# Two layers of SSM convolution and GEGLU on one core: DFT tables with half samples, and two filter blocks transformed by even and odd tokens between the layers' matmuls

## The chip, the core and the metric

The kernel runs on one core of a Trainium2 chip. The metric is device time in microseconds of one launch; the kernel before takes 943.9 us (median of 3 runs, 942.08 to 944.71). Its engines are named as in the profile: PE (TensorE's matmuls) and PEld (its weight loads), DVE (VectorE), ACT (ScalarE), POOL (GpSimd) and SP (SyncE, which here only issues DMAs). Each engine takes its own instructions in the order in which they were issued.

## What is computed

Two layers, each a gated long convolution over 2048 tokens and 576 channels and then a GEGLU feed-forward layer of width 4608. The inputs are bf16.

```python
def _A_ref(q, k, v, shift_k, ssm_k, ssm_D):        # ks = 4 taps
    k_shift = sum(k_pad[:, t:t + S, :] * shift_k[:, ks - 1 - t] for t in range(ks))
    kv = k_shift * v
    y = irfft(rfft(pad(kv, 2*S)) * rfft(pad(ssm_k, 2*S)))[:S]     # causal convolution, 2048 taps
    y = y + kv * ssm_D
    return q * y
def _B_ref(x, w_gate, w_up, w_down):
    return (_gelu(x @ w_gate) * (x @ w_up)) @ w_down

x = A_q
x = x + _A_ref(_layernorm(x), A_k, A_v, A_shift_k, A_ssm_k, A_ssm_D)
x = x + _B_ref(_layernorm(x), B_w_gate, B_w_up, B_w_down)
x = x + _A_ref(_layernorm(x), A_k, A_v, A_shift_k, A_ssm_k, A_ssm_D)
x = x + _B_ref(_layernorm(x), B_w_gate, B_w_up, B_w_down)
```

The convolution's y depends on k, v and the filter alone, so both layers share it.

## The kernel before

**Convolution.** The sequence is cut into four blocks of 512 tokens. The filter (with ssm_D added to its first tap) and kv are cut in the same way, and each block is taken to 512 frequencies by matmuls with sine tables that the kernel makes itself. Frequencies come in four tiles of 128 (`kt` 0 to 3), each with two parts `s`; tokens come as four rows `i` of 128 partitions. Output block m is the sum over blocks a of K[a] times H[m-a], a complex product on DVE (`prod`), and an inverse transform (`inverse`, L254) of 8 matmuls for each of four token tiles. Spectra wait in DRAM (`Hd` for the filter, `Kd` for kv).

Three tables are made before the feed-forward starts. `G` (1024 columns per row i) serves the filter: its token rows are contiguous, p + 128 i, which is what a DMA transpose from DRAM (`load_h`, L493) delivers. `F1` serves kv, whose token rows are interleaved, 4 p + i, and half of the inverse; `F2` serves the other half. `G`'s angles are made on DVE (`angles`, L117) and those of `F1` and `F2` on ACT (`f_angles`, L560); ACT makes the sines (L125).

There are two ways forward. `fwd_h` (L182) and `fwd_full` (L191) make one frequency tile and part from 8 matmuls of 288 columns. `fwd_eo` (L202) makes even and odd rows apart, 4 matmuls for 288 channels; sum and difference of the two (`cross`, L214) give the tiles kt and kt+2, so a block takes 8 groups of 4 where `fwd_h` takes 8 groups of 8.

**Start-up** (`begin`, L476, written out by hand). Filter block 0 is turned by TensorE transposes, blocks 1 to 3 by DMA transposes on SP's queue. Then come, on TensorE: filter block 0 (4 tiles), block 1 (tiles 0 and 2), kv block 0 by `fwd_full` (`kfwd`), the rest of block 1, block 2, the inverse of block 0, chunk 0's gate, norm and TensorE transposes (`gate0`, `root0`, `norm0`, `turn0`, `copy0`) mixed with the last tiles of blocks 2 and 3. k arrives for block 0 with its shifted rows from DRAM, in three DMAs (L141 to L143). The first 8 of block 1's 16 kv operations are done here (`kv1_ops`).

**Feed-forward.** Four chunks of 512 tokens in two layers are eight units, ordered (0,c0) (0,c1) (1,c0) (1,c1) (0,c2) (0,c3) (1,c2) (1,c3), and run in passes of 1, 2, 2, 2 and 1 units. A pass goes through F in three phases; a unit in a phase is here called a visit, so there are 24 (0 to 23). A visit has 216 gate/up matmuls (gu, L1116: 12 f-tiles of 18; each takes 64 rows, two lie side by side in the array) and 96 down matmuls (dn, L1132). ACT takes the gelu and DVE the product hT (L1121) of each f-tile; DVE adds each dn tile to x.

**What lies between.** The rest of the convolution (blocks 1 to 3, `step`, L275) and the norms are laid between these matmuls by a planner at build time. It keeps a clock per engine (`Pace`), costs for each operation (`C_...`) and queues: `Pq` for TensorE groups, `V` for DVE, `U` for the crosses after an even/odd group, `L` for loads, `aq` for ACT's statistics. After each f-tile and each dn step `fill` issues what fits. What it decides is fixed in the instruction order; TensorE takes convolution groups between f-tiles while `hurry` holds, and always between dn steps. `hurry` is over once chunk 1's y is there.

For a new unit, `prep` issues per token tile j: a product with y, a sum with x that also adds up its elements, a Square on ACT with the mean `nm` (from POOL, L834) as bias, the root on POOL, the norm `xn` on DVE (L903), and two DMA transposes on SP (`spread`, L933) that make xnT for gu.

Of the kernel before, what the change touches and what calls it, by code (L numbers as in the profile page):

```python
# [34 lines left out]
C_AC, C_AB = 0.76, 0.76  # L35
C_TT, C_ST, C_BN, C_NORM, C_HT, C_GELU, C_EVA, C_EVD = 0.76, 0.82, 0.47, 0.62, 0.69, 0.6, 0.66, 0.76
# [20 lines left out]
class Conv:  # L57
# [9 lines left out]
    def __init__(self, tc, ctx, pace, A_k, A_v, A_shift_k, A_ssm_k, A_ssm_D, ident, psp, cpsp, ypool):  # L67
# [6 lines left out]
        self.ident, self.psp, self.cpsp, self.ypool = ident, psp, cpsp, ypool  # L74
# [7 lines left out]
        self.prp = pool("c_pr", 3)  # L82
# [5 lines left out]
        self.F1 = self.cst.tile([P, RT, 2, 2, P], BF16, name="F1")  # L88
        self.F2 = self.cst.tile([P, 2, 2, 2, P], BF16, name="F2")
# [14 lines left out]
        self.V, self.L, self.Pq = deque(), deque(), deque()  # L104
# [12 lines left out]
    def angles(self, j, col, row, eng):  # L117
        for s, off in enumerate((3 * N4 // 4, 0)):
            eng.tensor_scalar(out=j[:, s, :], in0=col, scalar1=row, scalar2=float(off), op0=ALU.mult, op1=ALU.add)
# [8 lines left out]
    def load_k(self, b, eng):  # L128
# [10 lines left out]
        if b == 0:  # L139
            self.nc.vector.memset(k[0:1, 0:H, :], 0.0)  # L140
            eng.dma_start(out=flat[16:P, :], in_=rows(16 * RT + r0, P - 16))  # L141
            self.nc.gpsimd.dma_start(out=flat[1:16, :], in_=rows(RT + r0, 15))
            self.nc.gpsimd.dma_start(out=k[0:1, H:H + RT, :], in_=self.k2[0:RT, :].unsqueeze(0))  # L143
        else:
            eng.dma_start(out=flat[:], in_=rows(r0, P))
# [35 lines left out]

    def fwd_h(self, G, src, kt, s, dst):  # L182
        nc = self.nc
        ps = self.ps()
        for n, i in enumerate((2, 3, 0, 1)):
            for h in range(2):
                nc.tensor.matmul(ps[:, h, 0:HW], lhsT=G[:, i, s * NFQ + kt * P: s * NFQ + (kt + 1) * P],  # L187
                                 rhs=src[:, i, h * HW:(h + 1) * HW], start=(n == 0), stop=(n == RT - 1))
        nc.scalar.activation(out=self.halves(dst[:, s, :]), in_=ps[:, :, 0:HW], func=ACT.Copy, scale=1.0 / NFQ)

    def fwd_full(self, src, neg, kt, s, dst):  # L191

        nc = self.nc
        ps = self.ps()
        for i in range(RT):
            x = src[:, i, :] if kt < 2 or i % 2 == 0 else neg[:, i // 2, :]
            for h in range(2):
                nc.tensor.matmul(ps[:, h, 0:HW], lhsT=self.F1[:, i, s, kt % 2, :],  # L198
                                 rhs=x[:, h * HW:(h + 1) * HW], start=(i == 0), stop=(i == RT - 1))
        nc.scalar.copy(out=self.halves(dst[:, s, :]), in_=ps[:, :, 0:HW])  # L200

    def fwd_eo(self, src, kt, s, h):  # L202
# [3 lines left out]
        for e in range(2):  # L206
            for i in (e, e + 2):
                nc.tensor.matmul(ps[:, e, 0:HW], lhsT=self.F1[:, i, s, kt, :],  # L208
                                 rhs=src[:, i, h * HW:(h + 1) * HW], start=(i == e), stop=(i == e + 2))
        eo = self.eop.tile([P, 2, HW], F32, tag="eo", name="eo")  # L210
        nc.scalar.copy(out=eo[:], in_=ps[:, :, 0:HW])  # L211
# [39 lines left out]
    def lhs(self, kt, s, mt, F2):  # L251
        return self.F1[:, 2 * kt, s, mt // 2, :] if mt % 2 == 0 else F2[:, kt, s, mt // 2, :]
# [22 lines left out]
    def step(self, m, kv=None, loaded=False):  # L275
# [10 lines left out]
        if not loaded:  # L286
# [7 lines left out]
            self.L.append((lambda: self.kv_at.get(m - 1, NEVER), lk))  # L294
            self.L.append((lambda: self.fwd_at.get(m - 1, NEVER), lv))
# [34 lines left out]
        for kt, a in pairs:  # L330
            self.L.append((lambda a=a: max(self.hr_free[self.nhr % N_HR] if (m, a) != (1, 0) else 0.0,
                                           self.kr_free[self.nkr % 3] if a < m else 0.0),
                           load(kt, a)))
# [77 lines left out]
        for kt, a in pairs:  # L411
            for part in range(2):
                keys = [("ld", kt, a)] + ([("kc", kt % 2, s, h) for s in range(2) for h in range(2)] if a == m else [])
                self.V.append((lambda g=get(*keys): max(g(), self.pr_slot()), C_PR, v(kt, a, part)))
                if a > 0:
                    self.V.append((eo_done if a == 1 else lambda: 0.0, C_AC, add(kt, a, part)))
# [3 lines left out]
        for kt in range(2):  # L420
            for s in range(2):
                for h in range(2):
                    self.Pq.append((lambda: max(get("kv")(), NEVER if self.neo >= N_EO else 0.0), 0.49, fwd(kt, s, h)))
        def inv(mt):
            def run():
                self.yb = nyb
                self.inverse(m, mt, [(self.lhs(kt, s, mt, self.F2), z[(s, kt, mt % 2)])
# [8 lines left out]

    def pr_slot(self):
        return self.pr_free[self.npr % N_SM]

    def run_loads(self):  # L440
        t = self.t
        self.flush(t.pe)
        while self.L and self.L[0][0]() <= t.pe - 0.3:
            self.L.popleft()[1]()

    def run_v(self, limit):

        t = self.t
        if self.U and self.U[0][0] <= t.pe + 0.2 and max(t.dve, t.pe - 1.0) + self.U[0][1] <= limit:
# [26 lines left out]
    def begin(self, gate0, root0, norm0, turn0, copy0, x0_stats, more, scratch, wide, stay):  # L476

        tc, nc, D = self.tc, self.nc, self.D
        with ExitStack() as es:
            tmp = es.enter_context(tc.tile_pool(name="s_tmp", bufs=1))  # L480
            hp = es.enter_context(tc.tile_pool(name="s_h", bufs=2))
            sk1 = hp.tile([1, D, self.KS], BF16, tag="h", name="sk1")
            dvec = tmp.tile([1, D], BF16, name="dvec")
            ones = tmp.tile([1, P], BF16, name="ones")
            nc.vector.memset(ones[:], 1.0)
            nc.scalar.dma_start(out=sk1[:].rearrange("p d j -> p (d j)"), in_=self.sk.rearrange("d j -> (d j)").unsqueeze(0))
# [734 lines left out]
```

## Time and profile before

| What | us |
|---|---|
| Median of 3 runs | 943.9 |
| Profiled execution, its own time | 943.32 |
| Its span, first to last instruction | 941.5 |
| First gu matmul | 62.7 |
| PE busy in 0 to 20, 20 to 40, 40 to 60 | 15.48, 19.44, 16.46 |
| DVE busy in the same | 17.71, 19.29, 17.10 |
| ACT busy in the same | 16.34, 18.13, 12.15 |
| PE idle in 175 to 200 | 1.05 |

The profile lists each engine's busy time, the waits with the instruction that ended them, and the chain of work that ended last, followed back from the end. A line of the chain gives its start, its length and the instruction or DMA that the time belongs to. The busy time of an engine is no measure of what it is worth to shorten it: only work on that chain moves the end. The granted clock reads 1.00 throughout.

### The profile page before, as it was taken

Reading aid. Unit: us, or ns where it says so; the run is one execution under the profiler, and the core shown is the slowest. Engines: PE = TensorE matmul, PEld = TensorE weight load, DVE = VectorE, ACT = ScalarE, POOL = GpSimd, SP = SyncE. Lnnn points to the kernel's source line nnn. Section 1 sums busy time; section 2 is a strip of 40 time slices with the busy share of each in tenths; the row PEclk is TensorE's granted clock in tenths of the full one; section 3 lists DMA queues with packets and bytes.
Section 4 is the critical chain, followed back from the end, with each engine's and each line's share of the span. In section 5 each row is a group of like instructions: output and inputs, shape, how many; then the busy total and the mean of one; then the engine's idle time right before and its main releaser. Section 6 shows DMA issues by size and latency. Waiting matters only on the chain.

```text
span 941.5 us, 19061 instructions
## 1 busy us (share of the span) xinstructions
PE 926.9 (98%) x8128; PEld 536.5 (57%) x8128; DVE 571.4 (61%) x1027; ACT 295.9 (31%) x541; POOL 143.2 (15%) x303
## 2 busy tenths in 40 slices
PE   7989999999999999999999999999999999999998
PEld 5755564665655646546546556556556556556555
DVE  8977887898898637988982333663333335523332
ACT  8846214432124334231222421441221223311211
POOL 2453100511123104230100100230000002100000
PEclk9999999999999999999999999999999999999999
DMA  7989986765953522983930630891630630797720
GB/s 184 323 238 274 293 183 148 133 162 142 226 190 64 113 77 52 195 212 87 221 107 2 133 94 26 136 156 39 129 99 1 129 98 14 135 206 155 147 65 26
DMA packets 129065, 127.46 MB, mean 135 GB/s; under 512 B 45587, under 2 KB 121684, under 8 KB 128980
## 3 DMA queue, kind: packets, MB, share of 16 engines
q1 hardware_dynamic: 119904, 90.85, 45.7%
q0 software_dynamic: 8944, 34.49, 11.4%
q8 instruction: 63, 1.03, 0.5%
q10 hardware_dynamic: 132, 0.91, 0.4%
q14 instruction: 22, 0.18, 0.1%
HBM read 105.58 MB, written 10.62 MB: 123 GB/s over the span
## 4 chain that ended last, share of the span: by engine, by line
PE 91%; DMA 3%; DVE 2%; POOL 2%; ACT 1%; issue 1%; SPq 0%; POOLq 0%; DVEq 0%
PE gu L1116 59%; PE dn L1132 27%; DMA h<-in_A_ssm_k_dram 2%; PE cps L208 1%; PE cps L261 1%; PE ps L187 1%; DMA k<-in_A_k_dram 1%; POOL rstd L850 1%; PE ps L198 1%; DVE x_c L1161 0%; PE cps L187 0%; POOL ve L849 0%; ACT junk L842 0%; DVE x_c L877 0%; DMA xnT<-xn 0%
## 5 line engine op out<-in xcount | busy, mean ns | idle before, releaser
L1116 PE MATMUL gu<-xnT,wgu 64*128 64x512 bf16 x5184 | 565.5, 376 | 2.1 <-DVE x_c L1161 1.0
L1116 PEld LDWEIGHTS <-wgu 64*128 64x128 bf16 x5184 | 254.3, 94 | 305.2 <-issue 10.1
L1120 ACT ACTIVATE ga<-gu 128x512 f32<-128x512 f32 x288 | 171.9, 597 | 549.9 <-PE gu L1116 541.1
L1121 DVE TENSOR_TENSOR hT<-ga,gu 128x512 bf16<-128x512 f32 x288 | 197.6, 686 | 221.2 <-ACT ga L1120 219.7
L1132 PE MATMUL dn<-wd,hT 128*128 128x288 bf16 x2304 | 291.0, 286 | 0.5 <-DVE ob L1141 0.5
L1132 PEld LDWEIGHTS <-hT 128*128 128x128 bf16 x2304 | 223.5, 98 | 66.1 <-issue 10.5
L1166 DVE TENSOR_TENSOR x_c<-x_c,dn 128x576 f32<-128x576 f32 x64 | 48.2, 753 | 82.3 <-PE dn L1132 82.0
L834 POOL TENSOR_SCALAR nm<-s 128x1 f32<-128x1 f32 x60 | 21.1, 352 | 344.1 <-DVE x_c L1161 215.1
L842 ACT ACTIVATE junk<-x_c,nm 128x576 bf16<-128x576 f32 x48 | 37.0, 771 | 40.8 <-POOL nm L834 40.8
L327 POOL DMA_DIRECT2D hr<-Hd x32 | 17.3, 541 | 161.2 <-DVE prod L228 161.2
L850 POOL TENSOR_TENSOR rstd<-ve,neghalf_t 128x1 f32<-128x1 f32 x60 | 39.9, 665 | 5.0
L229 DVE TENSOR_TENSOR sum<-prod 128x576 bf16<-128x576 bf16 x72 | 33.0, 458 | 2.5
L187 PEld LDWEIGHTS <-G 128*128 128x128 bf16 x256 | 25.5, 100 | 11.2 <-issue 2.2
L187 PE MATMUL ps<-h,G 128*128 128x288 bf16 x192 | 27.6, 298 | 2.5 <-DMA h<-in_A_ssm_k_dram 1.7
L1152 DVE TENSOR_TENSOR ob<-x_c,dn 128x576 bf16<-128x576 f32 x15 | 11.2, 753 | 27.2 <-PE dn L1132 19.0
L163 DVE TENSOR_TENSOR kvt<-k,skc 128x1152 bf16<-128x1152 bf16 x32 | 23.9, 754 | 0.5
L849 POOL TENSOR_SCALAR ve<-ss 128x1 f32<-128x1 f32 x60 | 18.1, 301 | 32.4 <-ACT junk L842 32.3
L216 DVE TENSOR_TENSOR kc<-eo 128x288 bf16<-128x288 f32 x48 | 19.2, 453 | 2.1 <-ACT eo L211 2.1
L877 DVE SCALAR_TENSOR_TENSOR x_c<-g_t,rstd,x_c 128x576 f32<-128x576 f32 x16 | 13.1, 818 | 12.0 <-POOL rstd L850 11.9
L211 ACT COPY eo<-cps 128x576 f32<-128x576 f32 x24 | 15.3, 636 | 15.2 <-PE cps L208 12.7
L269 POOL DMA_DIRECT2D out_dram<-ob x12 | 6.7, 555 | 86.3 <-DVE ob L1152 86.2
L383 DVE TENSOR_TENSOR zs<-sum 128x576 f32<-128x576 bf16 x24 | 18.1, 755 | 0.5
(112 smaller groups left out, 464.7 us busy)
## 6 DMA issues: line engine op xcount, KB each, us to landing
wgu<-in_B_w_gate_dram SPq DMA_DIRECT2D x45, 576.0 KB, 5.7
wd<-in_B_w_down_dram SPq DMA_DIRECT2D x30, 864.0 KB, 6.7
wgu<-in_B_w_up_dram SPq DMA_DIRECT2D x45, 512.0 KB, 8.2
hr<-Hd POOLq DMA_DIRECT2D x32, 288.0 KB, 5.3
kr<-Kd POOLq DMA_DIRECT2D x24, 288.0 KB, 5.4
Hd<-h POOLq DMA_DIRECT2D x12, 288.0 KB, 4.6
Kd<-kc POOLq DMA_DIRECT2D x12, 288.0 KB, 6.6
k<-in_A_k_dram POOLq DMA_DIRECT2D x3, 1008.0 KB, 6.1
```

The source lines that it names most:

```text
L163: nc.vector.tensor_tensor(out=st[dst][:], in0=self.kt_[b][:, s0:s0 + 2, :], in1=self.skc[:, j, :].unsqueeze(1).to_broadcast([P, 2, D]), op ...
L187: nc.tensor.matmul(ps[:, h, 0:HW], lhsT=G[:, i, s * NFQ + kt * P: s * NFQ + (kt + 1) * P], rhs=src[:, i, h * HW:(h + 1) * HW], start=(n == ...
L216: self.nc.vector.tensor_tensor(out=dst, in0=eo[:, 0, :], in1=eo[:, 1, :], op=op)
L229: nc.vector.tensor_tensor(out=dst, in0=pr[:, 0, :], in1=pr[:, 1, :], op=ALU.subtract if part == 0 else ALU.add)
L834: nc.gpsimd.tensor_scalar(out=v["nm"][:], in0=v["s"][:], scalar1=-1.0 / D, scalar2=None, op0=ALU.mult)
L842: nc.scalar.activation(out=junk[:], in_=get_x(), func=ACT.Square, bias=v["nm"][:, 0:1], accum_out=v["ss"][:])
L850: nc.gpsimd.tensor_tensor(out=v["rstd"][:], in0=ve[:], in1=neghalf_t[:, 0:1], op=ALU.pow)
L1116: nc.tensor.matmul(pair[:, s, :], lhsT=w[r0:r0 + HK, k, gi * P:(gi + 1) * P], rhs=xnT[r0:r0 + HK, b, :], start=(k == 0), stop=(k == NKC - 1))
L1120: nc.scalar.activation(out=ga[:], in_=pair[:, 0, :], func=ACT.Gelu_apprx_tanh)
L1121: nc.vector.tensor_tensor(out=hT[:, fi, :], in0=ga[:], in1=pair[:, 1, :], op=ALU.mult)
L1132: nc.tensor.matmul(acc[:, h, 0:HW], lhsT=hT[:, fi, j * P:(j + 1) * P], rhs=wd[2 * wb + fi // WT][:, fi % WT, h * HW:(h + 1) * HW], start=( ...
L1166: nc.vector.tensor_tensor(out=xh, in0=xh, in1=acc[:, :, 0:HW], op=ALU.add)
```

## The change

One table `F` (rows 4 p + i, two frequency tiles, half samples) takes both filter and kv forward, and a table `I` holds all of the inverse. `G`, `F1` and `F2` go. The tiles 2 and 3 need the odd rows' sign turned; that now comes from a third, smaller table `neg` instead of negated data. All angles are made on DVE.

```diff
-    def fwd_h(self, G, src, kt, s, dst):
...
-    def fwd_full(self, src, neg, kt, s, dst):
+    def fwd_full(self, src, neg, kt, s, dst, scale=1.0):
...
+        for n, i in enumerate((1, 2, 3, 0)):
+            lhs = self.F[:, i, s, kt % 2, :] if kt < 2 or i % 2 == 0 else neg[:, i // 2, s, kt % 2, :]
...
+                nc.tensor.matmul(ps[:, h, 0:HW], lhsT=lhs, rhs=src[:, i, h * HW:(h + 1) * HW],
+                                 start=(n == 0), stop=(n == RT - 1))
+        nc.scalar.activation(out=self.halves(dst[:, s, :]), in_=ps[:, :, 0:HW], func=ACT.Copy, scale=scale)
```

Filter blocks 0 and 1 stay in the start-up. Both are loaded as they lie, on SP, and turned by 20 TensorE transposes each, with copies on ACT. k for block 0 comes in one DMA, issued first on ACT's queue (the taps `sk` follow it); its three shifted rows are made by matmuls with a shifted identity and copied by ACT. v, x of chunk 0 and the first weights follow on SP. Half of chunk 0's statistics move from DVE to ACT, and of the copies of chunk 0's transposed xn ACT takes the second half.

```diff
+            self.load_k(0, nc.scalar)
...
+            for r in range(KS - 2, -1, -1):
+                ps = self.ps()
+                for h in range(2):
+                    nc.tensor.matmul(ps[:, h, 0:HW], lhsT=self.shift, rhs=k[:, r + RT, h * HW:(h + 1) * HW], start=True, stop=True)
+                nc.scalar.copy(out=self.halves(k[:, r, :]), in_=ps[:, :, 0:HW])
...
+            def turn_h(b, g):
...
+                        nc.tensor.transpose(pt[:, i, db * P:db * P + w],
+                                            hn[b][0:w, db, :].rearrange("w (p i) -> w i p", i=RT)[:, 2 * g + i, :],
+                                            self.ident[0:w, 0:w])
+                nc.scalar.copy(out=hT[b][:, 2 * g:2 * g + 2, :], in_=pt[:, :, 0:D])
```

Block 1's kv operations all move into `step(1)`. Filter blocks 2 and 3 move out of the start-up: `step(2)` and `step(3)` call a new `hstep`, which loads the block with POOL's DMAs into the slot of k, de-interleaves it on ACT, turns it by five DMA transposes on SP, and takes it forward by `fwd_eo`, with the crosses on DVE into tiles of the `xn` pool and POOL's writes to `Hd`.

```diff
+    def hstep(self, b):
...
+            for c in range(nd + 1):
+                w = min(P, D - c * P)
+                nc.scalar.copy(out=hn[0:w, c, :].rearrange("w (i p) -> w i p", i=RT),
+                               in_=hn[0:w, c + 1, :].rearrange("w (p i) -> w i p", i=RT))
+                t.on_act(C_DEI, t.pe - 1.0)
+                nc.sync.dma_start_transpose(out=hT[:, :, c * P:c * P + w], in_=hn[0:w, c, :])
+            st["h_at"] = self.turned_at[b] = t.act + 12.0
...
+                eo = self.fwd_eo(st["h"], kt, s, h, 1.0 / NFQ)
...
+                        self.cross(eos[e], lo[:, cols], hi[:, cols])
...
+                    for k, x in ((kt, lo), (kt + 2, hi)):
+                        nc.gpsimd.dma_start(out=self.Hd[b][k][:, s * D:(s + 1) * D], in_=x[:])
```

The planner's loads of k and v for the next block wait for this, `hurry` now holds until the last chunk's y is there, and the Square takes the sum instead of the mean as its bias, with a scale:

```diff
-        hurry = lambda: (1, RT - 1) not in conv.y_at
+        hurry = lambda: (NCH - 1, RT - 1) not in conv.y_at
...
-            nc.scalar.activation(out=junk[:], in_=get_x(), func=ACT.Square, bias=v["nm"][:, 0:1],
+            nc.scalar.activation(out=junk[:], in_=get_x(), func=ACT.Square, bias=v["s"][:, 0:1], scale=-float(D),
...
-        aq.append((at_v(v, "nm_at"), C_SQ, run))
+        aq.append((at_v(v, "s_at"), C_SQ, run))
```

More of the change, by code (lines that the diff above doesn't have):

```diff
@@ L533, in taps @@
                 nc.scalar.copy(out=self.halves(self.skc[:, j, :]), in_=ps[:, :, 0:HW])
-            for i in range(RT):
-                j = tmp.tile([P, 2, NFQ], I32, tag="dft_j", bufs=2, name="dft_j")
-                self.angles(j, colv, rowh[:, i:i + 1], nc.vector)
-                self.mask(j[:])
-                self.sines(G[:, i, :], j[:].rearrange("p s f -> p (s f)"))
-                if i == 0:
-                    taps(3)
-                    taps(2)
-            taps(1)
-            taps(0)
@@ L662, in begin @@
             inv0(3)
-            more(2)
-            self.kv1 = self.kv_ops(1)
-            ops = iter(self.kv1)
-            def kv1_ops(n):
-                for _ in range(n):
-                    next(ops)[1]()
             gate0(0)
```

390 lines of the change are left out of this document (214 added, 176 removed).

## The prediction

> **What bounds the kernel now.** I read the page's busy time first, then the chain that ended last in order of time, then the stretches and the timeline where that chain isn't TensorE.
>
> ```profile
> PE 926.9 (98%) x8128; PEld 536.5 (57%) x8128; DVE 571.4 (61%) x1027; ACT 295.9 (31%) x541; POOL 143.2 (15%) x303
> ...
> PE 91%; DMA 3%; DVE 2%; POOL 2%; ACT 1%; issue 1%; SPq 0%; POOLq 0%; DVEq 0%
> ```
>
> TensorE is busy 98% of the span, so in the body of the kernel a matmul more is time more. The chain in order of time shows the rest:
>
> ```profile
> 37.05 15.08 DMA h<-in_A_ssm_k_dram
> 52.17 2.13 PE ps L187 x16
> ...
> 61.79 0.98 PE ps L187 x8
> 62.77 15.65 PE gu L1116 x144
> 78.42 0.59 PE cps L208 x4
> 79.02 2.05 PE gu L1116 x18
> ...
> 92.05 0.49 PE cps L208 x4
> ...
> 102.83 23.42 PE gu L1116 x216
> 126.24 11.87 PE dn L1132 x96
> ...
> 176.98 2.49 DMA xnT<-xn
> 179.60 23.27 PE gu L1116 x214
> ```
>
> The FFN starts at 62.77 us, held by a filter transpose (15.08) and the filter tiles behind it. A visit (one chunk, one third of F) is 23.42 + 11.87 = 35.29; 24 of them are 847.0. Of what is left after 62.77, the convolution's groups between visits take 3 x 7.84 = 23.5. A group of 4 costs 0.49 among dn matmuls (92.05), but among gu matmuls 0.59 to 0.60, and the 18 gu behind it take 2.05, not 23.42/12 = 1.95: 0.21 per place where gu is broken.
>
> ```profile
> 11.07 2.83 PE L187 MATMUL ps<-h,G 128*128 128x288 bf16 x12 [0.25 <-DVE h L554]
> 14.72 3.10 PE L187 MATMUL ps<-h,G 128*128 128x288 bf16 x24
> ...
> 42.74 0.82 DVE L801 SCALAR_TENSOR_TENSOR x_c<-x_b,mv,y 128x576 f32<-128x576 bf16 x1
> ...
> 166.45 11.80 SPq L933 DMA_TRANSPOSE xnT<-xn  x8
> ```
>
> From the timeline: the first filter matmuls take 0.236 each, later ones about 0.125; chunk 0's gate starts at 42.74; and chunk 1's eight xn transposes leave SP one after another, 2.95 per token tile, the first as soon as its xn exists (166.42). dn of that visit ends at 178.1, gu starts at 179.5: TensorE waits 1.4.
>
> **Body: what is certain.** Filter blocks 2 and 3 leave the start-up (there 128 matmuls) and come back as 8 even/odd groups of 4 each. 2 x 8 x 0.49 = **+7.84**, on TensorE, uncovered.
>
> Places: `hurry` now holds until the last chunk, and in the order of the changed kernel's TensorE instructions, 23 groups break a gu sequence (inverse 1: 3, filter 2: 4, inverse 2: 2, kv 3: 6, filter 3: 4, inverse 3: 4); before there are 8. 15 x 0.21 = **+3.15**.
>
> **Body: the edge before visit 3.** All 16 kv operations of block 1 now run in the FFN (before, 8 in the start-up): 8 x 0.754 = 6.0 us more VectorE work in visits 0 to 2, where its rows already add to about 35 of 35.29 per visit. So the inverses of chunk 1 slide by two gu groups, the last to behind the last gu. With G the end of visit 2's gu, before: first xn at G+0.2, next visit at G+13.3. After, VectorE's order is: last hT (ends G+1.5), mul and add of token tile 2 (0.82 + 0.90), first xn (0.76): G+4.0. Four pairs at 2.95 and 1.2 to land: G+17.0. dn ends at G+1.1+11.9 = 13.0. The wait is 4.0 in place of 1.4: **+2.6**. Bounds: 0 if SP's pairs shorten to their 2.5 of issue and VectorE is early, +3.6 if all of the slide counts.
>
> The square reads the sum itself as bias, so POOL's nm (0.35) and its hand-over leave the chain behind each layer. At the two exposed edges (600:625 and 785:802) TensorE idles 0.5 each: between 0 and -1.0; **-0.5**.
>
> **Body: costed at nothing.** VectorE gets 32 half crosses x 0.453 = 14.5, 7.2 in visits 4 and 5 and 7.2 in visits 9 and 10, where its rows then add to 21 to 32 of 35.29. ACT gets 16 evictions x 0.64 and 10 de-interleaving copies (128x512; between a 0.60 gelu and a 0.77 square), 17 us in visits where it is busy under a third. POOL gets 16 writes and 4 loads at 0.55, and loses 8 spills. SP gets 5 transposes per block, 18 column blocks where one xn pair has 9: 5.9 to issue, 2.5 to 3.4 to land (xn rows), behind the first copy (0.7): about 10. Between the last kv group and the first filter group stand 0.12 x 11.87 + 0.67 x 23.42 = 17 us of matmuls for block 2, about as much for block 3. If that cover fails TensorE itself waits, gu behind it; the weight loads queued behind these transposes on SP are needed a visit later.
>
> **Start-up.** Removed: the 1024-column table G (four angle sets, four sines), the twelve angle activations on ACT, two negations, three filter transposes from HBM (15.08 of path), 128 matmuls, two of four bn_stats sets. Added: 20 TensorE transposes, three shift products, four 128x1152 copies moved from DVE to ACT, two ACT statistics sets, half of the xnT copies on ACT. I follow the new order with old durations; back to back, ACT takes 0.53 per 128x576 (29.77 to 30.29) and 1.05 per sine.
> - k, then sk, on ACT's queue, beside hn on SP's: 1.18 MB before both are in; at 300 to 320 GB/s (2 to 6 us) from 2.0, they land at 6. Bounds: 2.2 (sk, first in the queue, was used at 2.16) and 10 (k took 9.4 beside the transposes).
> - ACT from 6.9: 4 taps (2.1), one sine (1.05), 3 shifted rows (1.6), 2 copies of 1152 (between 0.65 and 1.3 each; by the slope from 576 to 1024 elements, 1.2): 14.1. ACT, not k's arrival, sets this.
> - VectorE: angles (8 of 256 columns at 0.31 by the slope of its rows, 4 of 512 at 0.44) and 4 masks at 0.69 end at 8.5; then 4 products and 3 sums of 128x2304 at 1.36 (by the slope from 576 to 1152), the second held to 10.8 by the first shifted row, and 2 of 0.75: kv done at 20.4. Before, it was done at 24.7, so this is no longer in front.
> - Four h0 tiles at 1.96, the first at the half rate of the 11.07 row (3.9): TensorE done 24.0; ACT, with the negative sine, statistics (1.7) and an inverse sine in between, at 25.9.
> - ACT turns block 1's filter (2.4), then the first kv tile: 29.3. VectorE has its two bn_stats sets (1.23 each) done at 22.9, and waits.
> - From the first product to the first gate: before, 29.53 to 42.74 less a mask (0.69), 12.5; after, ACT's copies of h1 stand ahead of y: 13.5. First gate at 42.9.
> - Gates 4 x 1.65, norms 4 x 0.76, half copies 4 x 0.49 on VectorE, the last transpose (0.68): 12.2. First gu at **55.1**.
>
> Gain 62.8 - 55.1 = **-7.7**. Bounds: 48.2 (below) and 59 (sk at 10).
>
> [...]
>
> **Sum.** -7.7 + 7.84 + 3.15 + 2.6 - 0.5 = +5.4. The profiled execution took 943.3 (span 941.5), 0.6 under the median of the runs, 943.9. **Forecast 948.7**, 0.5% slower. A change under 0.3% (2.8 us) can't be told from none here: faster is under 941.1, slower over 946.7.
>
> **Rivals.**
> 1. *VectorE, not ACT, sets the start-up* (faster). If sk lands at 2.2 and the 1152 copies cost 0.65, h0 can start by 10 and end at 18, the second transpose by 20.4, just as kv is done; statistics 22.9, products and pairs 12.5, gates 12.2: 47.6. With no growth at the edge: -15.2 + 7.84 + 3.15 - 0.5 = -4.7, **938.6**. It decides once gu starts before 49.5 (46.9 if the edge grows as forecast). For: VectorE was busy 19.3 of the 20 us from 20 to 40 and sheds 10 us. Against: ACT's start-up work after the change, counted back to back, is about 41 us, and much of it stands in front of a TensorE group. 0.15.
> 2. *Half of that*: sk early, but copies slow, gu at 53, edge +1: -9.8 + 7.84 + 3.15 + 1 - 0.5 = +1.7, **945.0**, no change. 0.20.
> 3. *Cold array at the first gu*: the nearest row by state (half rate from 9.68, over by 13.7) would cost 4.0 x 0.5 = 2.0: **950.7**. The nearest by place speaks against it: after 48 to 52 us, where TensorE was busy 1.5 of 4, 16 matmuls took 2.13, the full rate; so it isn't in the sum. 0.10.
> 4. *The filter transposes come late*: 5 at the longest issue (2.7) and landing (8.9) seen, plus 0.7, are 23 against 17, for each of two blocks: +12, **960**; for one, 954.7. 0.10.
> That the change doesn't do what it says is excluded for TensorE by its instruction order.
>
> **Numbers.** Forecast 0.45, its own range 946.7 to 952.5 (the edge between 0.6 and 3.6, gu between 53.5 and 57.5). Faster 0.15 (rival 1), same 0.20, slower 0.65. Rival 1's near half and rival 4's near half bound the range: 940.5 to 955.
>
> **What would show it.** First gu near 55 with ACT nearly full from 20 to 45 us, and VectorE idle before the first product; 23 short interruptions of gu, 2.05 per 18 behind each; a wait of about 4 us after visit 2's dn with SP's transposes in front; no wait at the first filter group in visits 4 and 9. Wrong: gu before 50, or TensorE waiting on hT.

## The result and the profile after

The changed kernel takes 954.2 us (median of 4 runs, 953.54 to 954.34). Beside the kernel before on the same chip the ratio is 1.0113, 95% interval 1.0096 to 1.0131. The kernel before, with a fourth run, has a median of 943.4; the changed one is 10.8 us slower, where 5.4 was forecast. That is outside the forecast's own range (946.7 to 952.5) and just inside the outer one (940.5 to 955). The profiled execution took 954.34, its span is 952.6, 11.0 over the span before.

First the page's busy times, the clock in 40 slices and the chain by engine, of the changed kernel:

```profile
PE 932.0 (98%) x8090; PEld 532.4 (56%) x8090; DVE 576.5 (61%) x1035; ACT 305.5 (32%) x554; POOL 154.2 (16%) x316
...
PEclk9979999999999999999999999999999999999999
...
PE 89%; DVE 3%; POOL 3%; ACT 2%; DMA 1%; issue 1%; SPq 1%; ACTq 0%; DVEq 0%
```

38 matmuls fewer than before, and 5.1 us more of busy TensorE. The third slice (47.6 to 71.4 us) is at 7 tenths of the clock. That is new; the page before has 9 throughout. The list of TensorE's waits adds:

```profile
PE xps L1071 <- DVE xn L1060: 5.8, 3, 3.2
PE ps L582 <- DMA sk<-in_A_shift_k_dram: 3.1, 1, 3.1
PE gu L1174 <- DVE x_c L1219: 2.7, 2, 1.9
PE dn L1190 <- DVE hT L1179: 1.1, 1, 1.1
...
PE gu L1174 <- DMA xnT<-xn: 1.1, 1, 1.1
```

(Columns: us in total, times, longest.) The first two belong to the start-up. The third is 1.9 ahead of visit 3 and 0.82 in visit 8, the fourth is in visit 9, the last ahead of visit 3 again. (The third wait is put down to VectorE, but its instruction ends at 173.2 and gu starts at 173.81; the view does not name what came last.) The chain in order of time, for the start-up and for one visit with filter groups:

```profile
32.39 0.99 PE cps L189 x8
33.38 0.02 issue
33.41 0.65 ACT kc L191
...
41.41 0.55 ACT y L254
41.96 0.03 issue
41.99 0.83 DVE x_c L845
...
231.66 0.60 PE cps L199 x4
232.26 2.05 PE gu L1174 x18
```

The chain stays on TensorE's forward groups from 13.36 to 33.38, and ACT carries it from 33.41 to the first gate at 41.99. VectorE had waited 5.24 us for its first product:

```profile
28.25 0.76 DVE L216 TENSOR_TENSOR prod<-kc,h 128x1152 bf16<-128x1152 bf16 x1 [5.24 <-ACT kc L191]
```

The first gu starts at 55.71 (62.71 before). In the body the forecast picture is there: 0.60 for a group of 4 that breaks a gu sequence, 2.05 for the 18 gu behind it.

To see where the rest went I divide TensorE's timeline into visits, from the first gu of a visit to that of the next. Without convolution work a visit is 35.28; eight groups of 4 between dn matmuls make it 39.20.

| us | before | changed | difference |
|---|---|---|---|
| first gu | 62.71 | 55.71 | -7.00 |
| visit 0 | 40.05 | 41.02 | +0.97 |
| visit 1 | 35.28 | 35.28 | 0 |
| visits 2 and 3 | 80.55 | 83.93 | +3.38 |
| visits 4 to 13 | 364.59 | 379.21 | +14.62 |
| from visit 14 to the last matmul | 354.98 | 354.22 | -0.76 |
| sum | | | +11.21 |

The table shows one execution of each kernel. Six kernels, this one and five of those below, have the same instruction order up to the first gu (the changed kernel, late_rows, switches, no_filter, late_kv8, late_lead), and there the first gu comes between 54.05 and 55.71.

### The profile page after: what moved, and what is told of

It reads as the page before. It is cut to its first block, busy times and chain, and to the rows that moved or that the text cites. A ratio compares the mean times of both kernels' runs of the same rounds, so it can differ in the third digit from the quotient of the medians.

```text
span 952.6 us, 19068 instructions
## 1 busy us (share of the span) xinstructions
PE 932.0 (98%) x8090; PEld 532.4 (56%) x8090; DVE 576.5 (61%) x1035; ACT 305.5 (32%) x554; POOL 154.2 (16%) x316
## 3 DMA queue, kind: packets, MB, share of 16 engines
q8 instruction: 63, 1.03, 0.5%
## 4 chain that ended last, share of the span: by engine, by line
PE 89%; DVE 3%; POOL 3%; ACT 2%; DMA 1%; issue 1%; SPq 1%; ACTq 0%; DVEq 0%
PE gu L1174 57%; PE dn L1190 25%; PE cps L199 2%; PE ps L189 1%; POOL rstd L896 1%; PE cps L252 1%; ACT junk L888 1%; DVE x_c L923 1%; DVE x_c L1219 1%; POOL ve L895 1%; DMA xnT<-xn 1%; SPq L977 1%; PE hps L634 0%; POOL nm L880 0%; DMA sk<-in_A_shift_k_dram 0%
## 5 line engine op out<-in xcount | busy, mean ns | idle before, releaser
L1174 PE MATMUL gu<-xnT,wgu 64*128 64x512 bf16 x5184 | 571.8, 378 | 4.7 <-DVE x_c L1219 2.7
L1190 PEld LDWEIGHTS <-hT 128*128 128x128 bf16 x2304 | 223.9, 98 | 65.9 <-issue 10.1
L888 ACT ACTIVATE junk<-x_c,s 128x576 bf16<-128x576 f32 x48 | 37.1, 772 | 42.4 <-DVE x_c L923 26.9
L896 POOL TENSOR_TENSOR rstd<-ve,neghalf_t 128x1 f32<-128x1 f32 x62 | 43.3, 698 | 5.2
L202 ACT ACTIVATE eo<-cps 128x576 f32<-128x576 f32 x40 | 26.0, 651 | 25.3 <-PE cps L199 17.7
L895 POOL TENSOR_SCALAR ve<-ss 128x1 f32<-128x1 f32 x62 | 20.3, 328 | 28.2 <-ACT junk L888 25.8
L199 PEld LDWEIGHTS <-F 128*128 128x128 bf16 x160 | 14.3, 98 | 10.6 <-issue 7.5
L378 DVE TENSOR_TENSOR zs<-zs,sum 128x576 f32<-128x576 f32 x24 | 18.1, 756 | 0.6
L163 DVE TENSOR_TENSOR kvt<-k,skc 128x1152 bf16<-128x1152 bf16 x24 | 17.8, 754 | 0.3
L189 PEld LDWEIGHTS <-F 128*128 128x128 bf16 x144 | 14.8, 104 | 5.6 <-issue 0.9
```

The costliest lines, as they stand in the source:

```text
L189: nc.tensor.matmul(ps[:, h, 0:HW], lhsT=lhs, rhs=src[:, i, h * HW:(h + 1) * HW], start=(n == 0), stop=(n == RT - 1))
L199: nc.tensor.matmul(ps[:, e, 0:HW], lhsT=self.F[:, i, s, kt, :], rhs=src[:, i, h * HW:(h + 1) * HW], start=(i == e), stop=(i == e + 2))
L202: nc.scalar.activation(out=eo[:], in_=ps[:, :, 0:HW], func=ACT.Copy, scale=scale)
L888: nc.scalar.activation(out=junk[:], in_=get_x(), func=ACT.Square, bias=v["s"][:, 0:1], scale=-float(D), accum_out=v["ss"][:])
L895: nc.gpsimd.tensor_scalar(out=ve[:], in0=v["ss"][:], scalar1=1.0 / D ** 3, scalar2=EPS, op0=ALU.mult, op1=ALU.add)
L896: nc.gpsimd.tensor_tensor(out=v["rstd"][:], in0=ve[:], in1=neghalf_t[:, 0:1], op=ALU.pow)
```

## The experiments

All times are medians; the ratio is to the kernel before on the same chip, with its 95% interval, and "less" without another kernel's name is against the changed kernel's 954.2. The experiments ran on four chips, on which the kernel before took 942.8 to 943.5. Where two intervals overlap (warm_start and the changed kernel; late_warm, late_gate and late_gate2 against late_rows) the medians do not tell the two kernels apart, and the argument rests on the visits in the profiles. The text after each edit is what was put down before the run.

### Matmuls that keep the array at work

The granted clock by stretch shows what is special about visit 0, which is slow although nothing waits in it. Of the changed kernel, windows over the gate stage and visit 0's beginning (columns: window, its length, then busy time and count of PE, PEld, DVE, ACT, POOL, then granted clock, DMA share, GB/s):

```profile
44.00:48.00 4.00, 1.13 (x10) 0.67 (x7) 3.12 (x7) 2.83 (x7) 2.91 (x5) 1.00 0.30 85
48.00:52.00 4.00, 1.20 (x15) 1.03 (x16) 3.17 (x8) 1.38 (x4) 3.64 (x7) 0.64 1.09 371
52.00:56.00 4.00, 3.15 (x26) 2.25 (x25) 2.76 (x8) 2.16 (x4) 3.83 (x8) 0.50 1.11 346
56.00:60.00 4.00, 4.00 (x24) 1.65 (x23) 0.00 (x0) 0.44 (x2) 1.70 (x4) 0.58 0.97 360
```

TensorE is busy 2.3 of the 8 us from 44 to 52; the clock falls to 0.50 at about 49 and is back at 1.00 at about 59.3, behind 3.6 us of gu without a break. The same happens ahead of visit 3 (0.85, 0.50, 0.80 in the windows from 174 to 180). But DMA share is high beside it, so contention was a rival.

```diff
+        def warmth(n):
+            wm = cpsp.tile([P, 2, 512], F32, tag="cps", name="wm")
+            src = conv.I[:, 0, 0, :, :].rearrange("p m q -> p (m q)")
+            for _ in range(n):
+                nc.tensor.matmul(wm[:, 0, 0:HW], lhsT=conv.F[:, 0, 0, 0, :], rhs=src[:, 0:HW], start=True, stop=True)
...
+            if j in (0, 2):
+                warmth(12 if j else 8)
             pt = turned[j] = psp.tile([P, 2, 1024], BF16, tag="pr", name="xps")
...
             xnT = xnT_of[ui]
             end = ph == NP - 1
+            if (ui, ph) == (1, 0):
+                warmth(24)
```

The last two lines, at the start of visit 3, are in warm_all only.

> The changed kernel plus 20 matmuls (128x128 by 128x288, their result read by nobody) that keep TensorE at work in the two waits of the gate stage: 8 ahead of the first token group's transposes, 12 ahead of the third's. Theory (the array goes into visit 0 at half clock because it stood idle from 45.1 to 48.4 us): granted clock 1.00 from 48 to 62 us, the first gu still at 55.2 to 55.9, visit 0's 216 gu matmuls in 23.4 us instead of 25.30, the whole 1.9 us faster than the changed kernel, about 952.3. Rival (visit 0 is slowed by the weight transfers that run beside it, DMA share 1.0 to 1.1 from 48 to 62): the 216 take 25.3 as before and the time stays at 954.2, or is up to 1 us longer through the added matmuls.

Measured: 953.01 (1.0101, 1.008 to 1.0121), 1.2 less, where 1.9 was expected. Visit 0 takes 39.51, as expected, 1.5 less than in the changed kernel. In visit 9 of this profile dn waits 2.1 us for hT, 1.0 more than in the changed kernel.

> As the run before, and 24 more such matmuls (2.9 us at full clock) ahead of the first gu of visit 3, where PE waits 1.89 and 1.07 us. Theory: granted clock 1.00 from 172 to 180 us, the 214 gu that follow in 23.3 instead of 24.95, so 1.7 us more than the run before: about 950.6, 3.6 under the changed kernel. Rival (that edge is slow because the transposed tiles arrive late and the transfers run beside it): the 214 still take 24.9 and the time is that of the run before, 952.3 or above.

Measured: 951.03 (1.0073, 1.0054 to 1.0093), 3.2 less. The same windows, and those of the edge:

```profile
48.00:52.00 4.00, 4.00 (x27) 3.00 (x26) 3.08 (x8) 1.30 (x4) 3.51 (x7) 0.57 1.09 372
52.00:56.00 4.00, 2.62 (x36) 1.80 (x36) 2.49 (x7) 1.93 (x4) 4.00 (x8) 1.00 1.06 336
56.00:60.00 4.00, 4.00 (x40) 2.14 (x38) 1.82 (x3) 1.11 (x2) 0.95 (x2) 1.00 0.99 389
...
176.00:178.00 2.00, 2.00 (x22) 0.93 (x20) 1.33 (x4) 1.47 (x4) 0.48 (x2) 1.00 0.02 9
```

With the same DMA share (1.06, 0.99) the clock is 1.00 and visit 0 takes 39.51: contention is out. The size fits too. In the changed kernel, in late_rows and in switches (both below, with the same start-up) the half clock lasted 3.6, 3.3 and 5.6 us behind the first gu, and visit 0 took 41.02, 40.84 and 42.02: each time 39.20 and half of that stretch. One part of the expectation failed. The clock still fell, at 48 to 52, because the added matmuls waited 2.6 us for an eviction by ACT and started too late to prevent it (47.32, the fall was at 48.29); they only brought the clock back before gu came. Visit 3 takes 40.39 instead of 42.14, but the 24 matmuls (3.10 us) pushed its start back, so visits 2 and 3 together gain only 0.76.

### Where TensorE takes convolution groups

```diff
-        hurry = lambda: (NCH - 1, RT - 1) not in conv.y_at
+        hurry = lambda: (1, RT - 1) not in conv.y_at
```

This puts back the condition of the kernel before under which groups are laid between f-tiles. (The expectation words it as a priority of VectorE's work; its numbers are for this edit.)

> The changed kernel with the one condition set back by which the layers' own VectorE work goes ahead of the inverse's (it ends when the output blocks 0 and 1 are made, not 3). By the order of instructions 3 breaks of a gu sequence by convolution groups are left of 23, and the same 8090 matmuls run. Theory (a break costs 0.21 us): 20 x 0.21 = 4.2 us faster, about 950.0, less whatever waits the later layer-1 work makes. Rival (a break costs nothing, the groups' 0.49 us is all): 954.2 within 0.5, and the body's extra is in waits.

Measured: 946.98 (1.0031, 1.0018 to 1.0043), 7.2 less, more than either theory said. Visits 4 and 13, which in the changed kernel have four breaks and no wait, go from 40.05 to 39.20 both: 0.85 for four breaks, 0.21 each. Over visits 4 to 13 it is 379.21 to 372.68, 6.5: 4.2 for 20 breaks, 1.9 for the waits in visits 8 and 9, which are gone, and 0.4 left over. So the waits hung on the same condition. In the changed kernel's timeline of VectorE they look like this (columns: start, length, engine, line, operation, tiles, count, idle before and its releaser):

```profile
427.53 1.56 DVE L207 TENSOR_TENSOR half<-eo 128x288 bf16<-128x288 f32 x4
429.01 0.68 DVE L1179 TENSOR_TENSOR hT<-ga,gu 128x512 bf16<-128x512 f32 x1
431.60 0.46 DVE L207 TENSOR_TENSOR half<-eo 128x288 bf16<-128x288 f32 x1 [1.91 <-DMA xnT<-xn]
433.83 1.20 DVE L207 TENSOR_TENSOR half<-eo 128x288 bf16<-128x288 f32 x3 [1.78 <-DMA xnT<-xn]
434.94 2.10 DVE L1179 TENSOR_TENSOR hT<-ga,gu 128x512 bf16<-128x512 f32 x3
```

The half crosses take tiles of the xn pool; a tile is free when SP's transposes have read it. The crosses wait 1.91 and 1.78 us for that, three hT queue behind them, and dn waits 1.11 for hT. With the groups between dn steps instead, VectorE's crosses wait 0.64 at most in that visit, for ACT's evictions, and TensorE not at all.

What a break is made of was tried by itself, on the kernel with the condition set back (`seen` counts visits from 1, so 11 is visit 10; P is 128 rows, HK 64):

```diff
+        SWITCH = {11: (1, P), 13: (1, HK), 15: (8, P), 17: (8, HK)}
...
+                if len(seen) in SWITCH and fi < 6:
+                    n_mm, rows = SWITCH[len(seen)]
...
+                    for _ in range(n_mm):
+                        nc.tensor.matmul(wm[:, 0, 0:HW], lhsT=conv.F[0:rows, 0, 0, 0, :], rhs=src[0:rows, 0:HW],
+                                         start=True, stop=True)
```

> late_rows with breaks put into four visits that have none, after each of their first 6 gu groups (18 matmuls of 64 rows): visit 10 one matmul of 128 rows by 288 columns, visit 12 one of 64 rows by 288, visit 14 eight of 128 rows, visit 16 eight of 64 rows (results read by nobody; 0.1225 us each at 288 columns). A visit without a break takes 35.28. Theory (what costs 0.21 is the change from 64-row to 128-row matmuls and back): visit 10 37.28, visit 12 36.0, visit 14 42.4, visit 16 41.2. Rival (any other group between two gu costs it, by its new weights and output bank): visit 12 37.3 and visit 16 42.4. Rival (it grows with the number of matmuls, no price of the break): visit 10 36.0, visit 14 well above 42.4 or at 41.2.

Measured, by visit: 37.29, 36.01, 42.44 and 41.16, all within 0.05 of the theory (the whole: 961.88, ratio 1.0191, 1.017 to 1.0213). In TensorE's timeline, visit 10 and then visit 12:

```profile
445.09 0.30 PE L1189 MATMUL wm<-I,F 128*128 128x288 bf16 x1
445.32 2.12 PE L1177 MATMUL gu<-xnT,wgu 64*128 64x512 bf16 x18
447.37 0.30 PE L1189 MATMUL wm<-I,F 128*128 128x288 bf16 x1
447.60 2.12 PE L1177 MATMUL gu<-xnT,wgu 64*128 64x512 bf16 x18
```
```profile
519.64 0.28 PE L1189 MATMUL wm<-I,F 64*128 64x288 bf16 x1
519.74 2.32 PE L1177 MATMUL gu<-xnT,wgu 64*128 64x512 bf16 x19
521.71 0.28 PE L1189 MATMUL wm<-I,F 64*128 64x288 bf16 x1
```

From one added matmul to the next it is 2.28 us in the first (447.37 - 445.09) and 2.07 in the second (521.71 - 519.64). The lengths of single rows overlap; only the distances tell. The price belongs to the change from 64 rows to 128 and back, not to the group and not to its size. It is 0.21 us for both ways together; what in that change takes the time, no run here shows.

### The filter groups left out

```diff
-            self.hstep(m)
+            self.turned_at[m] = self.hfwd_at[m] = 0.0
+            self.hx_at[m] = 0.0
...
-                nc.gpsimd.dma_start(out=hr[(kt, a)][1][:].rearrange("p s d -> p (s d)"), in_=self.Hd[m - a][kt])
+                nc.gpsimd.dma_start(out=hr[(kt, a)][1][:].rearrange("p s d -> p (s d)"), in_=self.Hd[min(m - a, 1)][kt])
```

> The changed kernel without the forward transforms of filter blocks 2 and 3 in the body (no loads, copies, transposes, 16 even/odd groups, crosses and stores for them): the inverse takes block 1's spectrum in their place, so output blocks 2 and 3 are computed with other numbers. Start-up is unchanged. By the order 9 breaks of gu sequences are left of 23. Theory: 7.84 (groups) + 14 x 0.21 = 2.9 (breaks) + 1.1 (the down projection of visit 9 behind the half crosses) + perhaps 0.8 (visit 8's follow-up) = 11.8 to 12.6 faster, about 942. Rival (the filter groups are hidden, and the loss against the forecast is the clock and the edges alone): at most 4 us faster, 950 or above.

Measured: 944.09 (0.9997, 0.9983 to 1.0012), 10.1 less. The groups are not hidden. It gains less than the theory said since the planner's new order has waits of its own in visits 8 and 9 (0.71 and 2.12): over visits 4 to 13 the difference is 10.15, which is 7.84 + 14 x 0.21 + 1.93 - 2.83 = 9.9. Without any filter work in the body the start-up's gain would thus be used up by the clock, the edge and those waits: this kernel has the gain and stands level with the kernel before.

Its profiled execution took 941.20, the shortest of the twelve. In it the clock fell at 46.32 and was back at 1.00 at 53.15, ahead of the first gu at 54.05, and visit 0 took 39.51 with no matmul added. So the fall does not cost visit 0 the same in every execution: 0 here, 2.8 in switches, with one instruction order.

### The edge ahead of visit 3

```diff
-        conv.step(1, loaded=True)
+        conv.step(1, kv=conv.kv_ops(1)[8:], loaded=True)
```

On top of late_rows. The kernel leaves out the first 8 of block 1's 16 key-value operations (the 24 of the expectation is a slip), so its outputs from block 1 on are wrong numbers.

> late_rows without the first 8 of the 24 key-value operations of block 1 in the body (8 x 0.76 us of VectorE; the outputs that hang on block 1 come from unfinished sums). By the order of instructions there are 9 breaks instead of 3. Theory (the edge ahead of visit 3 is late because VectorE now has these in the body, and the fall of the clock there comes from that longer wait): the wait ahead of visit 3 goes from 2.94 to about 1.2 us, the clock holds 1.00 there, visit 3 takes 40.2 to 40.4 instead of 42.04, and with 6 x 0.21 for the breaks the sum is about 2.2 under 947.0: 944.8. Rival (the edge is set by the chain over VectorE, GpSimd and ScalarE behind the inverse, whatever VectorE did before): the wait stays 2.9, and the time is 947 to 948.3.

Measured: 943.23 (0.9989, 0.9976 to 1.0002), 3.75 less than late_rows. Visit 0, with five breaks, takes 1.2 more; visits 2 and 3 take 79.26 instead of 83.87, and of the wait nothing is left, where 1.2 was expected:

```profile
165.83 7.15 PE L1190 MATMUL dn<-wd,hT 128*128 128x288 bf16 x57
172.91 5.35 PE L1174 MATMUL gu<-xnT,wgu 64*128 64x512 bf16 x48
```

So 8 x 0.76 = 6 us of VectorE work, two visits earlier, decide a wait of 2.94, and through it the clock. If so, room on VectorE must do the same with all the work in. In late_rows VectorE idles 0.5 to 1.0 ahead of 11 of the 24 hT of visits 1 and 2 (the expectation's "nearly every" is too many); a product of 0.76 is not issued there:

```diff
-HOLD, LEAD = 14.0, 1.8
+HOLD, LEAD = 14.0, 2.4
```

> late_rows with one planning constant changed, the slack past the next gu group up to which VectorE is given convolution work: 2.4 instead of 1.8 us. VectorE idles 0.5 to 1.0 us ahead of nearly every gating product in visits 1 and 2 of late_rows; a product of 0.76 then fits there. By the order of instructions the inverse of block 1 comes two gu groups (4 us) earlier in visit 2, with 4 breaks instead of 3. Theory (the edge ahead of visit 3 and the fall of the clock there are block 1's rows coming late through VectorE's work): the wait of 2.94 goes under 1.2, no granted clock of 0.5 in visit 3, visits 2 and 3 together 4 us shorter than 83.86, and with +0.2 for the break about 943.2. Rival (the edge is a chain over GpSimd and ScalarE with a length of its own): wait 2.9, time 947.2.

Measured: 944.06 (1.0005, 0.9994 to 1.0017). Visits 2 and 3 take 79.33, no wait. That is 4.5 of 4.0 expected; but visits 4 to 13 take 374.60 instead of 372.68, 1.9 given back.

### Putting it together

First late_rows and warm_all together, with fewer matmuls at the edge:

```diff
-                warmth(24)
+                warmth(12)
```

> The condition set back as in late_rows, and the added matmuls of warm_all together, but 12 instead of 24 ahead of visit 3 (24 took 3.1 us there and pushed its first gu back by 1.0). Theory (breaks and waits, and the clock, are separate terms): late_rows' 947.0, less 1.5 in visit 0 and 1.75 in visit 3: about 943.7, the granted clock 1.00 throughout. Rival (the terms share a cause, so that one is got back only once): 945.5 or above.

Measured: 945.97 (1.003, 1.0018 to 1.0043), by the ratio level with late_rows (1.0031), as the rival said. Its reason is not the rival's, though. Visit 0 keeps its gain (39.51). At the edge 12 matmuls were too few: TensorE still idled 1.17 and 1.03 us there, the clock fell (0.64 and 0.51 in the windows from 172 to 176), and visit 3 took 41.99.

The gate stage itself has two idle stretches of VectorE, 0.74 and 0.73, both waiting for the root on POOL. POOL's `ve` of the first token group is queued behind `nm` of the second, and a store of a filter spectrum (0.73 in the chain) stands in front of the third. The edit, on top of late_warm, moves the roots up and the store behind the stage:

```diff
-                self.flush(0.0)
+                if (b, kt) != (1, 3):
+                    self.flush(0.0)
...
             gate0(0)
+            root0(0)
             gate0(2)
-            root0(0)
+            root0(2)
             h1(3)
             gate0(1)
+            root0(1)
             norm0(0)
             turn0(0)
-            root0(2)
             gate0(3)
+            root0(3)
...
```

> late_warm with GpSimd's small operations of the gate stage in another order: each token group's nm, variance and power follow its gate at once instead of behind the next group's nm, the store of a filter spectrum that stands between them goes behind the stage, and VectorE normalises the first group after the third gate operation pair. Theory (VectorE's two idle stretches of 0.74 and 0.73 us in that stage are waits for GpSimd's queue): VectorE has no idle from 41.5 on, the first gu comes 1.5 to 1.7 us earlier, about 53.4, and the kernel takes about 942.1. Rival (what VectorE has to do up to visit 3 sets the edge there): the first gu comes earlier but the wait ahead of visit 3 grows by as much, 943.7.

Measured: 945.93 (1.002, 1.0009 to 1.0032). Neither theory: the first gu came at 54.15, not earlier than in late_warm (53.97). VectorE's two waits for POOL were gone, but the added matmuls, held until 46.45 by ACT's eviction and then mostly at half clock (from 46.68), made VectorE wait 0.69 and 1.22 for TensorE's transposes. So they were replaced, and those at the edge left out:

```diff
-            if j in (0, 2):
-                warmth(12 if j else 8)
             pt = turned[j] = psp.tile([P, 2, 1024], BF16, tag="pr", name="xps")
+            for _ in range({0: 18, 2: 12, 1: 6}.get(j, 0)):
+                nc.tensor.transpose(pt[:, 0, 0:P], ident[:], ident[:])
```

> late_rows with the gate stage's order of late_gate, and in place of its added matmuls 18, 12 and 6 transposes of the identity into the tile that the next token group's transposes fill (0.075 us each, they wait for no eviction; in late_gate the added matmuls waited until 46.45 for ScalarE's eviction and ran at half clock, so the copies waited 0.69 and 1.22 for TensorE). Theory: VectorE idles no more than 0.3 us between 41 and 53, the first gu comes 1.5 earlier behind the first gate operation than in late_rows, the granted clock stays 1.00 from 44 to 60 and visit 0 takes 39.5: about 3.0 under 947.0 if the edge ahead of visit 3 does not take it back, 944.0. Rival (VectorE's work up to visit 3 sets that edge): the wait there grows from 2.94 by 1.5 to 3, and the time is 946 to 947.

Measured: 944.81 (1.0022, 1.0012 to 1.0031). The first gu comes at 53.55 (55.30 in late_rows), the clock stays at 1.00 from 44 to 60, visit 0 takes 39.51. Of these 3.1 us the edge ahead of visit 3 takes back 0.6 (a wait of 3.54 instead of 2.94; the clock still falls there, 0.57 from 172 to 176), and the median falls by 2.2: mostly the theory, a little of the rival. The new order and the added transposes were not tried one by one, so which of them holds the clock up is open.

Then both, on top of late_gate2:

```diff
-HOLD, LEAD = 14.0, 1.8
+HOLD, LEAD = 14.0, 2.4
```

> The two runs before together. Theory (one takes away what the other would run into): 946.98 less 3.0 and less 3.8: 940.2, under the kernel before. Rival (the edge stays VectorE's, so the two give what the larger gives): 943 or above.

Measured: 943.42 (1.0001, 0.9991 to 1.0011). The first gu at 53.50 and the edge (80.19 in visits 2 and 3) are as hoped, visits 4 to 13 are not: 376.22. The key-value groups now stand among visit 7's dn matmuls:

```profile
355.15 1.14 PE L1193 MATMUL dn<-wd,hT 128*128 128x288 bf16 x8
358.30 0.65 PE L199 MATMUL cps<-v,F 128*128 128x288 bf16 x4 [2.01 <-ACT eo L202]
358.79 1.31 PE L1193 MATMUL dn<-wd,hT 128*128 128x288 bf16 x8
```

A group waits 2.01 us for the eviction of the one before. Behind that wait the clock falls as well:

```profile
358.00:360.00 2.00, 1.70 (x13) 1.33 (x13) 1.64 (x4) 1.64 (x4) 1.84 (x5) 0.91 0.25 39
360.00:362.00 2.00, 2.00 (x10) 1.26 (x9) 0.70 (x1) 0.65 (x1) 1.10 (x3) 0.50 0.83 279
```

So visits 7 and 8 take 3.5 more than in late_rows. In late_lead, which has the same wait (2.00) and keeps the clock at 1.00 there, they take 1.9 more; its ACT timeline shows a Square ahead of that eviction, and the Square waiting for VectorE. The slack helps where VectorE is the limit, in visits 0 to 2, and harms later. So 2.4 holds only while `hurry` does, and `LEAD` goes back to 1.8:

```diff
-                fill(t.pe + C_GU + LEAD, hurry(), conv.left > 0)
+                fill(t.pe + C_GU + (2.4 if hurry() else LEAD), hurry(), conv.left > 0)
```

> late_both with the slack of 2.4 us only until output blocks 0 and 1 are made (visits 0 to 2), 1.8 from there on. In late_both visits 7 and 8 took 82.19 us together where late_rows needs 78.66: key-value groups stood in visit 7's down projections and waited 2.01 us for an eviction that ScalarE had queued behind a Square, which waited for VectorE. Theory (that wait comes from the slack outside visits 0 to 2): visits 7 and 8 together 78.7 again, the rest as in late_both, so 943.4 less 3.5: 939.9, under the kernel before by 0.3%. Rival (the wait comes from the earlier phase of the body, as visit 4 starts 6.8 us earlier): 943 again.

Measured: 939.22 (0.9958, 0.9941 to 0.9974): 4.1 us under the kernel before, 15.0 under the changed one. Visits 7 and 8 take 78.40 together, visits 4 to 13 372.43. All the work of the change is in it. Its waits:

```profile
PE ps L582 <- DMA sk<-in_A_shift_k_dram: 3.1, 1, 3.1
PE xps L1074 <- DVE xn L1061: 3.0, 3, 1.4
...
PE gu L1177 <- DMA xnT<-xn: 0.6, 1, 0.6
```

In the gate stage the longest wait is 1.4 instead of 3.2, ahead of visit 3 there is 0.6 left, and the granted clock is 1.00 from 17.2 us, where its records begin, to the last matmul.

## Why the forecast was wrong in size

| Term | forecast | measured | how |
|---|---|---|---|
| first gu | -7.7 | -7.0 | 62.71 to 55.71 (-7.0 to -8.7 in the six kernels with this start-up) |
| filter groups | +7.84 | +7.84 | two blocks of 3.92 x 2 in the visits |
| 15 more breaks | +3.15 | +3.15 | 0.21 each (late_rows, switches) |
| wait ahead of visit 3 | +2.6 | +1.9 | 1.05 to 2.96 |
| nm off the chain | -0.5 | -0.76 | visits 14 to 23 |
| half clock in visit 0 | 0 (rival 3: +2.0) | +1.8 | 41.02 less 39.20 (0 to 2.8 with this start-up) |
| half clock in visit 3 | 0 | +1.7 | its gu matmuls 24.95, before 23.27 |
| waits in visits 8 and 9 | 0 | +1.9 | 0.82 and 1.11 |
| rest | | +0.7 | |
| sum | +5.4 | +11.2 | to the last matmul; +11.0 by the spans, +10.8 by the medians |

**The terms in the sum held.** The start-up went as worked out: the first product at 28.25 (forecast 29.3), the first gate at 41.99 (42.9), ACT in front of it from 33.41 on and TensorE before that. Only the gate stage was 1.5 us longer than its 12.2, through POOL's queue; late_gate2, with another order there, comes down to 11.6 (41.94 to 53.55). Rival 1 (VectorE sets the start-up) is refuted by the chain and by VectorE's 5.24 us of waiting, and its half (gu at 53) by the first gu. Rival 4 (filter transposes late) didn't show: no TensorE wait stands in front of the first filter groups.

**The step that failed is rival 3, "so it isn't in the sum".** I priced the half rate rightly (+2.0 against 1.8) and put it aside by one row: 16 matmuls at the full rate behind a stretch of 48 to 52 us in which TensorE was busy 1.5 of 4. The windows of the kernel before:

```profile
44.00:48.00 4.00, 4.00 (x35) 3.19 (x34) 3.61 (x8) 2.92 (x6) 2.41 (x4) 1.00 1.20 225
48.00:52.00 4.00, 1.54 (x17) 1.06 (x14) 3.23 (x8) 3.02 (x6) 3.85 (x8) 1.00 1.04 200
```

The changed gate stage is emptier for longer, 1.13 and 1.20 in the same two windows, and from 45.1 to 51.5 only nine transposes (0.68 us) stand in it. The row spoke for one length of idling and was used for another. (The 1.00 that is noted for the kernel before speaks only for the time from 13.56 us on: there its clock's records begin, and the half rate of the 11.07 row ends.) That an emptier gate stage lets the clock fall, nothing of the kernel before showed; the changed kernel's windows do, and then the fall has to be looked for at every edge that is made longer: the wait ahead of visit 3, which I did forecast, cost nearly as much again through the clock. The two falls make 3.5 of the 5.8 us that the sum lacks, the waits in visits 8 and 9 (below) 1.9. With one fall the forecast would have been rival 3's 950.7, and 952.4 with both (1.7 from the row above). From the first gu to the full rate it was 3.6 us in the changed kernel (55.71 to about 59.3) and at visit 3 3.5 (175.28 to about 178.8); in switches it was 5.6 (54.19 to 59.83).

**"Costed at nothing" failed in part.** The half crosses had room on VectorE by its busy share, as said. But they take their tiles from the xn pool, so they wait for SP's transposes with hT behind them; the forecast named the cover that TensorE has, not what the crosses wait for. That these waits and the breaks are one thing, and both hang on `hurry`, was seen only in late_rows; the 15 breaks were counted as a price of the change, though they belong to one condition in it, and setting it back saved 7.2 us.

**The edge** was put down to the 8 key-value operations and SP's transposes. late_kv8 shows the first; its size (1.9) is under the 2.6. (The prediction's 1.4 for the kernel before counts two gu matmuls in the gap; TensorE's idle time there is 1.05.) SP's share was not tried by itself. The remaining 0.7 us of the sum, about 0.2 in visit 8 and 0.4 in visit 9, I did not trace.

## What to carry to other kernels

Where TensorE is the bound, ask of each wait that grows whether the array will be at full rate behind it: in the changed kernel the waits in the gate stage and ahead of visit 3 cost 1.8 and 1.7 us more behind them. Such a cost can differ between executions: with one instruction order visit 0 lost 0 in no_filter and 2.8 us in switches, and the mean granted clock of no_filter's 12 runs lies between 0.990 and 0.995. So read the clock in more than one. Where small groups go between matmuls with another number of rows, count the breaks in the instruction order, since each cost 0.21 us here (128 rows among 64), with one matmul in the group or eight, and put the groups where the number is the same already. Work that is moved to an engine with a low busy share still needs its buffers and its place in that engine's queue: look at what its first instruction waits for, and at the next edge that engine feeds.

## What the hardware showed that I had not expected

The clock falls without TensorE being quite idle: in the changed kernel with 0.68 us of transposes between 45.1 and about 49.1, in late_warm with 2.2 us of idle time that two gu matmuls divide, at the edge. Idle stretches of 1.40, 0.95 and 0.64 us with transposes between them (late_gate2) left it at 1.00. Transposes of the identity, in a stage whose order had been changed too, went with a clock that held (1.00 from 44 to 60 in late_gate2), and they waited for nothing; in no_filter the clock came back behind a stretch with nothing but transposes in it (3.08 us busy from 49.73 to 53.15). Matmuls that had to wait 2.6 us for their output bank came too late, ran in part at half rate themselves and delayed what stood behind them.

Nor does the length of a wait decide by itself: 2.0 us brought the fall in late_both and not in late_lead. In the trace of the changed kernel the clock's records begin at 18.38 us and change at 49.10, 59.34, 175.39 and 178.81: 30.72, 10.24, 116.05 and 3.41 us apart, which is 9, 3, 34 and 1 times 3.413. In no_filter, with the same instruction order up to the first gu, the changes at 46.32 and 53.15 are 6.83 apart, twice as much. So I counted stretches of 3.41 us on from such places in each trace; here are some at full clock, with the time that TensorE was busy in them:

| Run | stretch | busy | clock in the next stretch |
|---|---|---|---|
| late_gate2, edge | 168.63 to 172.04 | 0.39 | 0.50 |
| changed kernel | 45.69 to 49.10 | 0.68 | 0.50 |
| late_warm, edge | 169.15 to 172.57 | 1.39 | 0.50 |
| late_both, visit 7 | 356.21 to 359.63 | 1.41 | 0.50 |
| no_filter, visit 9 | 401.31 to 404.72 | 1.51 | 1.00 |
| switches, edge | 172.47 to 175.89 | 1.54 | 0.50 |
| late_gate2 | 45.75 to 49.16 | 1.69 | 1.00 |
| late_lead, visit 7 | 358.76 to 362.18 | 1.80 | 1.00 |
| kernel before | 47.69 to 51.11 | 1.85 | 1.00 |

The wait of late_both lies in one stretch; that of late_lead is divided between two (3.03 busy in the one ahead). In these rows 1.41 us or less goes with a fall and 1.69 or more with none; between them 1.51 went with none (no_filter) and 1.54 with a fall (switches). That is read off these traces; no run was made to test it.
